# Layer scale on one core: blocks of 60, 60 and 8 rows in place of 8, 60 and 60, and the first 7.9 MB load goes ahead of gamma

## The chip, the cores and the metric

The kernel runs on one core of a Trainium2 chip. The metric is the device time of one execution in microseconds (us). Before the change the median of three runs is 119.92 us (119.86 to 119.98). The profiled execution took 119.96 us, of which 118.6 us lie between its first and its last instruction; the profile calls this the span, and every position in time below counts from its start.

## The reference

```
B, S, D = 1024, 16, 512
x, y:  bfloat16 [B, S, D]        gamma: bfloat16 [D]
def reference(x, y, gamma):
    return x + gamma * y
```

There is one multiplication and one addition for each element. x and y are 16.8 MB each and so is the output: 33.56 MB are read and 16.78 MB are written. No element is used twice.

## The kernel before, in words

The 16,384 rows of 512 elements are spread over the 128 partitions, so that each partition owns 128 rows of 1 KB. `BLOCKS` cuts these 128 rows in three blocks, here of 8, 60 and 60 rows. Inside a block each partition's rows lie one after the other in memory, so one transfer of a block is 128 pieces of contiguous memory, of 8 KB each for the 8-row block (1 MB in all) and of 60 KB each for a 60-row block (7.9 MB in all). All of y has a place of its own in on-chip memory (`y_sb`, 128 rows), and the result is written over it. x has a buffer of 75 rows (`x_sb`), so the rows of x share slots, and a later load of x has to wait for an addition that frees its slots.

Nothing is planned by a scheduler: the order is written out by hand in four lists.

- `SP` is the list of the loads, which the Sync engine issues in this order. `('y', 8, 68)` is rows 8 to 68 of y, and the fourth entry of an x load is the slot in `x_sb` where it begins. A load of x waits on the semaphore `s_add` for the additions that free its slots (L132).
- `ACT` is the list of the Scalar engine's queue: the load of gamma (1 KB, L129), then three stores (L138). A store waits for the additions on its rows. The first store also waits for `s_go`, which TensorE gives when the load named in `RELEASE`, the last big load of x, has landed.
- `DVE` is the list of VectorE's work on the pieces in `PIECES`: 'm' multiplies a piece of y by gamma in place (L180), 'a' adds x to it (L189). Blocks and pieces have the same edges, except that one 60-row block is cut in pieces of 15 and 45 rows.
- `EARLY` says how many entries of the two queues are moved to the very front of the program, ahead of the barrier with which the engines begin. In the kernel before these are the first two loads of y.

After the early loads the Sync queue waits at its third entry, the Scalar queue waits before gamma, and VectorE waits before its first multiplication. TensorE releases all three when the load named in `HOLD`, the 1 MB of y, has landed (`s_held`, L149). Then gamma is loaded as one row into `gamma_row`. TensorE multiplies it by a column of ones, which copies it to all partitions of PSUM (L152), and VectorE casts it into `gamma_sb` (L154). From there the list `DVE` runs.

At the end the Sync engine waits for all additions and all stores.

Of the kernel before, what the change touches and what calls it, by code (L numbers as in the profile page):

```python
# [3 lines left out]

BLOCKS = [8, 60, 60]

PIECES = [8, 15, 45, 60]


SP = [
    ('y', 0, 8),
    ('y', 8, 68),
    ('x', 8, 68, 0),
    ('y', 68, 128),
    ('x', 68, 128, 15),
    ('x', 0, 8, 0),
]
ACT = [('g',), ('s', 8, 68), ('s', 68, 128), ('s', 0, 8)]  # L20

EARLY = (2, 0)

HOLD = ('y', 0, 8)

RELEASE = ('x', 68, 128, 15)

DVE = [('m', 0), ('m', 1), ('m', 2), ('a', 2), ('a', 1), ('m', 3), ('a', 3), ('a', 0)]
MULT, ADD = mybir.AluOpType.mult, mybir.AluOpType.add


def _take(sem, n, eng):


    return eng.wait_ge(sem, n).then_inc(sem, -n)  # L35


def kernel(
    tc: tile.TileContext,
    x: bass.AP,  # L40
    y: bass.AP,
    gamma: bass.AP,
    out: bass.AP,
):

    nc = tc.nc
    P = nc.NUM_PARTITIONS
    tc.close()  # L50
    tc.compile()  # L51

    xf = x.flatten_outer_dims()
    yf = y.flatten_outer_dims()
    of = out.flatten_outer_dims()
    N, D = xf.shape
    rows = N // P
    n = len(PIECES)
    assert sum(PIECES) == rows
    starts = [sum(PIECES[:c]) for c in range(n + 1)]  # L60
    dt = xf.dtype
    edges = [sum(BLOCKS[:c]) for c in range(len(BLOCKS) + 1)]
    assert edges[-1] == rows

    def rows_of(t, a, b):

        c = max(c for c in range(len(BLOCKS)) if edges[c] <= a)
        assert b <= edges[c + 1]
        block = t[P * edges[c] : P * edges[c + 1]].rearrange("(p n) d -> p n d", p=P)
        return block[:, a - edges[c] : b - edges[c], :]  # L70

    gamma_row = nc.alloc_sbuf_tensor("gamma_row", [1, D], dt).ap()
    ones_row = nc.alloc_sbuf_tensor("ones_row", [1, P], dt).ap()
    gamma_sb = nc.alloc_sbuf_tensor("gamma_sb", [P, D], dt).ap()
    y_sb = nc.alloc_sbuf_tensor("y_sb", [P, rows, D], dt).ap()
    x_loads = [w for w in SP + ACT if w[0] == "x"]
    y_loads = [w for w in SP + ACT if w[0] == "y"]
    stores = [w for w in SP + ACT if w[0] == "s"]
    for loads in (x_loads, y_loads, stores):
        assert sum(w[2] - w[1] for w in loads) == rows  # L80
    x_rows = max(w[3] + w[2] - w[1] for w in x_loads)
    x_sb = nc.alloc_sbuf_tensor("x_sb", [P, x_rows, D], dt).ap()
    gamma_ps = nc.alloc_psum_tensor("gamma_ps", [P, D], mybir.dt.float32).ap()

    sem = nc.alloc_semaphore
    s_gamma, s_ones, s_ps, s_dve = sem("s_gamma"), sem("s_ones"), sem("s_ps"), sem("s_dve")
    s_load = {w: sem("s_" + "_".join(map(str, w[:2]))) for w in x_loads + y_loads}
    s_held = {nc.sync: sem("s_held_sp"), nc.scalar: sem("s_held_act"), nc.vector: sem("s_held_dve")}
    s_add, s_go, s_rel, s_end, s_out = sem("s_add"), sem("s_go"), sem("s_rel"), sem("s_end"), sem("s_out")
    added = [a for kind, *a in DVE if kind == "a"]  # L90
    order = {a[0]: k for k, a in enumerate(added)}

    def meets(a, b, c, d):
        return a < d and c < b

    def pieces_of(a, b):
        return [c for c in range(n) if meets(starts[c], starts[c + 1], a, b)]

    def x_at(row):
        return next(w[3] + row - w[1] for w in x_loads if w[1] <= row < w[2])  # L100

    def frees(w):

        c = set()
        for v in x_loads[: x_loads.index(w)]:
            lo, hi = max(v[3], w[3]), min(v[3] + v[2] - v[1], w[3] + w[2] - w[1])
            if lo < hi:
                c |= set(pieces_of(v[1] + lo - v[3], v[1] + hi - v[3]))
        return sorted(c)

    early = []

    def ring(eng, what, n_early):

        known, went = 0, False
        for k, w in enumerate(what):
            kind = w[0]
            if k == n_early:
                _take(s_held[eng], 1, eng)
            need = frees(w) if kind == "x" else pieces_of(w[1], w[2]) + list(w[3:]) if kind == "s" else []  # L120
            need = max((order[c] + 1 for c in need), default=0)
            if kind == "s" and not went:
                _take(s_go, 1, eng)
                went = True
            if need > known:
                eng.wait_ge(s_add, need)
                known = need
            if kind == "g":
                i = eng.dma_start(out=gamma_row, in_=gamma.unsqueeze(0)).then_inc(s_gamma, 16)  # L129
            elif kind == "x":  # L130
                to = x_sb[:, w[3] : w[3] + w[2] - w[1], :]
                i = eng.dma_start(out=to, in_=rows_of(xf, w[1], w[2])).then_inc(s_load[w], 16)  # L132
            elif kind == "y":
                r = slice(w[1], w[2])
                i = eng.dma_start(out=y_sb[:, r, :], in_=rows_of(yf, w[1], w[2])).then_inc(s_load[w], 16)
            else:
                r = slice(w[1], w[2])
                i = eng.dma_start(out=rows_of(of, w[1], w[2]), in_=y_sb[:, r, :]).then_inc(s_out, 16)  # L138
            if k < n_early:
                early.append(i.ins)  # L140

    ring(nc.sync, SP, EARLY[0])
    ring(nc.scalar, ACT, EARLY[1])


    nc.vector.memset(ones_row, 1.0).then_inc(s_ones, 1)  # L146
    _take(s_load[HOLD], 16, nc.tensor)
    for s_one in s_held.values():
        nc.tensor.sem_inc(s_one, 1)  # L149
    _take(s_ones, 1, nc.tensor)  # L150
    _take(s_gamma, 16, nc.tensor)
    nc.tensor.matmul(gamma_ps, ones_row, gamma_row, start=True, stop=True).then_inc(s_ps, 1)  # L152
    _take(s_ps, 1, nc.vector)
    nc.vector.tensor_copy(out=gamma_sb, in_=gamma_ps).then_inc(s_dve, 1)  # L154
    _take(s_dve, 1, nc.vector)

    _take(s_load[RELEASE], 16, nc.tensor)
    nc.tensor.sem_inc(s_go, 1)
    nc.tensor.sem_inc(s_rel, 1)

    landed, open_mults = set(), 0

    def need(loads, c):
        for w in loads:
            if w not in landed and meets(starts[c], starts[c + 1], w[1], w[2]):
                if w == RELEASE:
                    _take(s_rel, 1, nc.vector)
                elif w == HOLD:
                    _take(s_held[nc.vector], 1, nc.vector)
                else:  # L170
                    _take(s_load[w], 16, nc.vector)
                landed.add(w)

    for kind, *args in DVE:
        c = args[0]
        yt = y_sb[:, starts[c] : starts[c + 1], :]
        if kind == "m":
            need(y_loads, c)
            g = gamma_sb[:, None, :].to_broadcast([P, PIECES[c], D])
            nc.vector.tensor_tensor(out=yt, in0=yt, in1=g, op=MULT).then_inc(s_dve, 1)  # L180
            open_mults += 1
        else:
            need(x_loads, c)
            if open_mults:
                _take(s_dve, open_mults, nc.vector)
                open_mults = 0
            at = x_at(starts[c])
            xt = x_sb[:, at : at + PIECES[c], :]
            nc.vector.tensor_tensor(out=yt, in0=xt, in1=yt, op=ADD).then_inc(s_add, 1)  # L189


    nc.scalar.sem_inc(s_end, 1)
    _take(s_end, 1, nc.sync)
    _take(s_add, n, nc.sync)
    _take(s_out, 16 * len(stores), nc.sync)

    main = nc.main_func.blocks[0].instructions
    names = {i.name for i in early}
    for b in nc.main_func.blocks[1:]:
        for i in [i for i in b.instructions if i.name in names]:  # L200
            b.instructions.remove(i)
    for k, i in enumerate(early):
        main.insert(1 + k, i)
# [30 lines left out]
```

## Time and profile before

| what | from the profile of before |
|---|---|
| time, median of three | 119.92 us |
| span | 118.6 us |
| VectorE busy | 70.1 us (59%), 10 instructions |
| TensorE busy | 0.6 us |
| memory read and written | 33.56 MB and 16.78 MB |
| multiplication or addition of 60 rows | 16.2 us |
| of 45 rows | 12.2 us |
| of 15 rows | 4.2 us |
| of 8 rows | 2.3 us |
| issue of the 60-row x load (rows 68 to 128) | at 53.60 us |
| issue of the first store | at 77.83 us |

The compute engines are listed with their busy time and its share of the span. The DMA (memory transfer) work is listed apart: 16 DMA engines move all bytes, each transfer is spread over all of them in packets, and a queue is the ordered list of transfers that one issuing engine has handed to them. Queue q1 belongs to the Sync engine and carries the loads of x and y; q10 belongs to the Scalar engine and carries gamma and the stores. A packet here is one partition's piece, 8 KB or 60 KB, or a 4-byte write to a semaphore. The trace records each packet with its start and its duration. What one DMA engine does in the whole kernel is 48 packets of 60 KB and 24 of 8 KB.

### The profile page before, as it was taken

The numbers are of one execution on the slowest core, as the hardware profiler recorded it, in microseconds if no ns is written. First come the engines' busy times: TensorE is split into PE (matmuls) and PEld (weight loads), VectorE is DVE, ScalarE is ACT, GpSimd is POOL, SyncE is SP. The second block draws the span as 40 slices with busy tenths as digits, with TensorE's granted clock in tenths as the row PEclk, the third lists the DMA queues.
The fourth block names the chain that finished last, engine by engine and source line by source line (L and its number), as shares of the span: only waits on it lengthen the run. The fifth ranks groups of instructions, "written<-read, shape, count | busy, mean of one in ns | idle before, by whom it ended". The sixth has DMA issues, their size and how long they took to land. (4 is left out here: it accounts for less than half of the span.)

```text
span 118.6 us, 87 instructions
## 1 busy us (share of the span) xinstructions
PE 0.6 (0%) x1; PEld 0.1 (0%) x1; DVE 70.1 (59%) x10; POOL 0.2 (0%) x4
## 2 busy tenths in 40 slices
PE   0001000000000000000000000000000000000000
PEld 0000000000000000000000000000000000000000
DVE  0000720199999399999499999569999950000000
POOL 0000000000000000000000000000000000000000
DMA  5999799779779879879977977897997797797787
GB/s 182 503 560 435 331 394 601 331 331 663 331 331 642 352 331 621 373 331 394 601 331 331 663 331 331 384 633 331 414 580 331 331 663 331 331 663 331 331 367 318
DMA packets 1298, 50.33 MB, mean 424 GB/s; under 512 B 145, under 2 KB 146, under 8 KB 146
## 3 DMA queue, kind: packets, MB, share of 16 engines
q1 hardware_dynamic: 864, 33.55, 65.8%
q10 hardware_dynamic: 434, 16.78, 32.7%
HBM read 33.56 MB, written 16.78 MB: 424 GB/s over the span
## 5 line engine op out<-in xcount | busy, mean ns | idle before, releaser
L180 DVE TENSOR_TENSOR y_sb<-y_sb,gamma_sb 128x4096 bf16<-128x4096 bf16 (+3 forms) x4 | 34.7, 8690 | 9.7 <-DVEq L35 9.7
L189 DVE TENSOR_TENSOR y_sb<-x_sb,y_sb 128x23040 bf16<-128x23040 bf16 (+3 forms) x4 | 34.6, 8688 | 4.5 <-DVEq L35 4.5
L154 DVE CAST gamma_sb<-gamma_ps 128x512 bf16<-128x512 f32 x1 | 0.7, 692 | 10.1 <-DVEq L35 10.1
L146 DVE MEMSET ones_row<- 1x128 bf16 x1 | 0.2, 165 | 2.0 <-PEq L51 2.0
L152 PE MATMUL gamma_ps<-gamma_row,ones_row 1*128 1x512 bf16 x1 | 0.6, 578 | 11.6 <-PEq L35 11.6
L152 PEld LDWEIGHTS gamma_ps<-gamma_row,ones_row 1*128 1x128 bf16 x1 | 0.1, 100 | 11.5 <-issue 11.5
L218 POOL MEMSET const-uint8-127<- 128x1 uint8 x1 | 0.1, 102 | 0.0
L218 POOL MEMSET const-bfloat16-1.0<- 128x1 bf16 x1 | 0.1, 101 | 0.0
L218 POOL MEMSET const-float32-0.0<- 128x1 f32 x1 | 0.1, 98 | 0.2 <-issue 0.2
L218 POOL MEMSET const-float32-1.0<- 128x1 f32 x1 | 0.1, 98 | 0.0
## 6 DMA issues: line engine op xcount, KB each, us to landing
y_sb<-in_y_dram SPq DMA_DIRECT2D x2, 7680.0 KB, 38.2
x_sb<-in_x_dram SPq DMA_DIRECT2D x2, 7680.0 KB, 29.9
out_dram<-y_sb ACTq DMA_DIRECT2D x2, 7680.0 KB, 21.0
y_sb<-in_y_dram SPq DMA_DIRECT2D x1, 1024.0 KB, 4.9
x_sb<-in_x_dram SPq DMA_DIRECT2D x1, 1024.0 KB, 22.3
out_dram<-y_sb ACTq DMA_DIRECT2D x1, 1024.0 KB, 22.1
gamma_row<-in_gamma_dram ACTq DMA_DIRECT2D x1, 1.0 KB
```

The lines of the kernel that those rows point to most:

```text
L146: nc.vector.memset(ones_row, 1.0).then_inc(s_ones, 1)
L152: nc.tensor.matmul(gamma_ps, ones_row, gamma_row, start=True, stop=True).then_inc(s_ps, 1)
L154: nc.vector.tensor_copy(out=gamma_sb, in_=gamma_ps).then_inc(s_dve, 1)
L180: nc.vector.tensor_tensor(out=yt, in0=yt, in1=g, op=MULT).then_inc(s_dve, 1)
L189: nc.vector.tensor_tensor(out=yt, in0=xt, in1=yt, op=ADD).then_inc(s_add, 1)
L218: nc = _bacc.Bacc("TRN2", target_bir_lowering=False, num_devices=1)
```

## The change

The first load becomes a 60-row block of y, alone at the front of the program. gamma no longer waits for a load of y; it goes out as soon as the Scalar engine has passed the barrier at the start. The other five loads wait until gamma has landed. The 8-row block moves from the front to the end of the list of loads. So the load named in `RELEASE`, which opens the stores, is now followed by two 1 MB loads in place of one, and VectorE multiplies and adds the 8-row piece last.

The purpose is to have gamma on the chip early, with work for the DMA engines meanwhile, and to let the stores be released while small loads are still to be moved.

```diff
-BLOCKS = [8, 60, 60]
+BLOCKS = [60, 60, 8]
-PIECES = [8, 15, 45, 60]
+PIECES = [15, 45, 60, 8]
 SP = [
-    ('y', 0, 8),
-    ('y', 8, 68),
-    ('x', 8, 68, 0),
-    ('y', 68, 128),
-    ('x', 68, 128, 15),
-    ('x', 0, 8, 0),
+    ('y', 0, 60),
+    ('x', 0, 60, 0),
+    ('y', 60, 120),
+    ('x', 60, 120, 15),
+    ('y', 120, 128),
+    ('x', 120, 128, 0),
 ]
-ACT = [('g',), ('s', 8, 68), ('s', 68, 128), ('s', 0, 8)]
-EARLY = (2, 0)
-HOLD = ('y', 0, 8)
-RELEASE = ('x', 68, 128, 15)
-DVE = [('m', 0), ('m', 1), ('m', 2), ('a', 2), ('a', 1), ('m', 3), ('a', 3), ('a', 0)]
+ACT = [('g',), ('s', 0, 60), ('s', 60, 120), ('s', 120, 128)]
+EARLY = (1, 0)
+AHEAD = 1
+RELEASE = ('x', 60, 120, 15)
+DVE = [('m', 0), ('m', 1), ('a', 1), ('a', 0), ('m', 2), ('a', 2), ('m', 3), ('a', 3)]
...
-            if k == n_early:
-                _take(s_held[eng], 1, eng)
+            if eng is nc.sync and k == AHEAD:
+                _take(s_held, 1, eng)
...
     nc.vector.memset(ones_row, 1.0).then_inc(s_ones, 1)
-    _take(s_load[HOLD], 16, nc.tensor)
-    for s_one in s_held.values():
-        nc.tensor.sem_inc(s_one, 1)
     _take(s_ones, 1, nc.tensor)
     _take(s_gamma, 16, nc.tensor)
+    nc.tensor.sem_inc(s_held, 1)
     nc.tensor.matmul(gamma_ps, ones_row, gamma_row, start=True, stop=True).then_inc(s_ps, 1)
...
                 if w == RELEASE:
                     _take(s_rel, 1, nc.vector)
-                elif w == HOLD:
-                    _take(s_held[nc.vector], 1, nc.vector)
                 else:
                     _take(s_load[w], 16, nc.vector)
```

## The prediction, made before the changed kernel was run

> **What bounds the kernel now.** I read the page from its second part on: the span in 40 slices, then the DMA queues, then the timeline, and last the packet records of the places where the order of transfers changes.
>
> ```profile
> DVE  0000720199999399999499999569999950000000
> DMA  5999799779779879879977977897997797797787
> GB/s 182 503 560 435 331 394 601 331 331 663 331 331 642 352 331 621 373 331 394 601 331 331 663 331 331 384 633 331 414 580 331 331 663 331 331 663 331 331 367 318
> q1 hardware_dynamic: 864, 33.55, 65.8%
> q10 hardware_dynamic: 434, 16.78, 32.7%
> HBM read 33.56 MB, written 16.78 MB: 424 GB/s over the span
> ```
>
> VectorE has holes, DMA has none. The two queues together are busy for 65.8 + 32.7 = 98.5% of 16 engines' span, 116.9 of 118.6 us. The swing between 331 and 663 GB/s comes from counting a packet where it ends. In the packet records a 60 KB packet takes 2.267 us, load or store, and the next starts 2.264 us after it; an 8 KB packet takes 0.309, the next starting 0.306 later. Each engine's work is therefore 48 x 2.264 + 24 x 0.306 = 108.7 + 7.3 = 116.0 us. The first packets start at 1.02 us, but those of half the engines need about a microsecond instead of 0.31 and end at 2.05 to 2.31, so the steady rate begins at about 1.74. 1.74 + 116.0 = 117.7; the engines end between 117.83 and 118.26, and the last store is reported 0.35 us later, at 118.61. So nothing between the first packet and the last costs more than half a microsecond, and the bound is the number of bytes at the engines' rate.
>
> ```profile
> 0.00 0.85 SPq L135 DMA_DIRECT2D y_sb<-in_y_dram  x2
> 5.23 0.33 SPq L132 DMA_DIRECT2D x_sb<-in_x_dram  x1
> 5.43 0.52 ACTq L129 DMA_DIRECT2D gamma_row<-in_gamma_dram  x1
> 11.57 0.58 PE L152 MATMUL gamma_ps<-gamma_row,ones_row 1*128 1x512 bf16 x1 [11.57 <-PEq L35]
> 53.60 4.40 SPq L132 DMA_DIRECT2D x_sb<-in_x_dram  x2
> 77.83 19.02 ACTq L138 DMA_DIRECT2D out_dram<-y_sb  x3
> ```
>
> In this timeline the reader is to see how far ahead transfers are issued. The x load of 53.60 waits for an addition; the load before it, of y, lands at 59.35. The stores are issued at 77.83, and the last load's packets end at 79.14 to 79.58 with the first store's following at once: the smallest margin of the kernel, and it just holds. The 12% "issue" in the chain of waits is the chain's lost track behind the stores' transfer, no cost of its own.
>
> **What the Trainium skill says.** "DMA: Bandwidth & Descriptors", section "Where 436 GB/s comes from", puts the ceiling of the 16 engines at 435 GB/s; the trace's 61,440 bytes in 2.264 us are 27.1 GB/s an engine, 434 for 16, which agrees. The same page, "Queues, rings and completion order", says an engine goes round-robin between the queues it has work for, a packet at a time. The trace agrees: gamma's 1 KB packet starts at 8.76 and its semaphore write at 11.07, with one 60 KB load packet in between. The same page, "Latency and other measured facts", gives 0.6 us to the first byte of a transfer issued from Sync or Scalar; here the first packet starts 1.02 us after its issue and the trace's figure is used. That page says nothing of the cost of alternating between stores and loads on one engine.
>
> **The change part by part.** *Bytes and packets:* the same six loads, three stores and gamma, with as many packets of each size. 116.0 us an engine before and after: 0.
>
> *The first load.* It is 60 rows instead of 8. The delay up to 1.74 us is that of the first bytes, which a larger packet has once too: 0. Half the engines showed 0.7 to 1.0 us too much on their first packet, so I allow 0.3 either way. Issuing one early load instead of two spares 0.43 us of Sync's time, hidden by the first load's packets.
>
> *gamma without a hold.* VectorE passes the barrier at 1.99, so gamma is issued at about 2.0 instead of 5.43. It took 6.0 us then from issue to landing (11.43), behind 60 KB packets; the same now lands it at about 8, one packet sooner or later 6 to 10. All that stands behind it fits under y's first load: that is 8 x 2.264 = 18.1 us of packets, to 19.85.
>
> *The hold of five loads until gamma has landed.* Queued behind it on Sync: all other loads; those who wait are the DMA engines and then VectorE. Release to issue took 0.33 us (4.90 to 5.23), issue to first packet 1.0, so x's first packets are ready at about 9.5, 11.5 at worst, against 19.85. Hidden by y's load by over 8 us: 0.
>
> *VectorE.* y lands at 1.74 + 18.1 + 0.35 = 20.2; multiplications of 15 and 45 rows run to 36.7. x lands at 38.3; the additions of 45 and 15 rows run from 38.5 to 50.7 and 54.9. The first frees the second big x load, issued at 50.8, first packet at 51.8; y's second load keeps the engines to 1.74 + 54.3 = 56.1, 4.3 us to spare. The last x load follows at 54.9. The 60-row multiplication runs 56.6 to 72.8. Moving the 8-row multiplication away from the front is free: VectorE was waiting there (7.6 us idle).
>
> *The stores.* The big x load has its last packets at 1.74 + 72.4 = 74.2, lands at 74.55; from landing to store issue was 0.35 (77.48 to 77.83), so issue at 74.9 and first packets ready at about 76.0. By then the 8 packets of y's 8 rows are done but for two; with x's 8, ten 8 KB packets an engine remain. Before, one 1 MB load covered this delay, barely; now two do. Nothing was lost there before, so nothing is gained. From 76.0 an engine alternates 2.26 us of store with 0.31 of load: the last x load, landing 2.5 us after the big one before, now lands at about 76 + 10 x 2.57 = 102. The 60-row addition (75.2 to 91.4) lets the second store go at 91.4, while the first lasts to about 97: 5 us to spare. The 8-row multiplication follows the big addition; its addition waits for x, ending at 104.5, and its store is wanted at 115.3: over 10 us to spare. The sum stays 0.
>
> *Alternation itself.* No row of before shows a load packet after a store packet on one engine. From below: 0, since load to store at 79.14 and load to gamma to load at 8.76 (46 ns) show no gap. From above: each of ten loads exposes a start as at the beginning, 0.7 us, 7 us in all. I take 0: the engine's rate is the same for both directions, and the one switch between queues back to a load cost nothing. For the range I keep 0.1 us a switch, 1 us.
>
> Sum: 119.92 + 0 = 119.9 us.
>
> **The rivals.** *First: loads between stores are slow.* For it: never seen before, and the kernel holds its stores until the big loads are in, which avoids nearly all mixing. Against it: free switches elsewhere. With 0.1 us for each of ten packets: 119.9 + 1.0 = 120.9 us, slower. *Second: a cleaner start or equal engines.* Engines differ by 0.43 us at the end, and the last has 0.28 us too much on 8 KB and 0.11 on 60 KB packets; if these go, it ends 0.39 earlier, 119.5 us, faster. For it: the excess is at the first transfer, which is replaced. Against it: the second to last engine ends only 0.09 earlier. *Third: a gap in the queue*, from gamma landing late or the second x load going out after 56. It needs a delay of 4 to 8 us; a gap of 1 us gives 120.9. The margins speak against it.
>
> **How the numbers follow.** No change 50%, slow alternation 26%, cleaner start 20%, a gap 4%. The likeliest is 119.9. The range runs from 119.5, the second rival, to 120.9, the first and the third at their stated size; left out are larger costs of alternation, about 13%, and little below. Faster by over 0.2% (under 119.68): 0.22, the second rival and a margin. Slower (over 120.16): 0.28, since the alternation can cost less than that. Same: 0.50.
>
> **What would show it.** Right: both queues again at 98 to 99%, 60 KB packets at 2.267, first store issued near 75, the 8 rows of x landing near 102 with no harm, last packet at about 118.2. Wrong: 8 KB packets longer than 0.31 us between stores, or gaps ahead of them (first rival); last packet before 117.9 (second); an empty slice near 20 or 56 us (third).

## The result, and the profile after

The changed kernel takes 121.10 us (median of six runs, 120.90 to 121.27) against 119.89 us (119.84 to 119.99). The ratio is 1.0098, with a 95% interval of 1.0085 to 1.0111: 1.2 us slower. The forecast was 119.9 us, with a range up to 120.9. So the time is outside the range, on the side of the first rival.

The page of the changed kernel, its span and its DMA queues (packets, MB, share of 16 engines' span):

```profile
span 119.8 us, 84 instructions
q1 hardware_dynamic: 864, 33.55, 66.1%
q10 hardware_dynamic: 434, 16.78, 32.4%
HBM read 33.56 MB, written 16.78 MB: 420 GB/s over the span
```

The number of packets and of bytes is that of before, and there is still no hole: 98.5% of the engines' span. But 66.1% of 119.8 is 79.2 us for the Sync queue's loads, against 65.8% of 118.6, 78.0 us, before. With the durations of the packet records added up it is 79.2 against 78.1 us an engine, and 38.8 us in both kernels for the other queue, that of the stores. The same load packets keep the engines about 1.1 us longer, and that is nearly the whole difference of 1.2 us. So the time is to be looked for in load packets that last longer, not in gaps.

Its timeline, with the lines that answer to those shown of before:

```profile
0.00 0.37 SPq L135 DMA_DIRECT2D y_sb<-in_y_dram  x1
1.43 0.52 ACTq L129 DMA_DIRECT2D gamma_row<-in_gamma_dram  x1
9.10 0.58 PE L150 MATMUL gamma_ps<-gamma_row,ones_row 1*128 1x512 bf16 x1 [9.10 <-PEq L35]
9.14 0.33 SPq L132 DMA_DIRECT2D x_sb<-in_x_dram  x1
51.53 0.33 SPq L132 DMA_DIRECT2D x_sb<-in_x_dram  x1
75.75 21.46 ACTq L138 DMA_DIRECT2D out_dram<-y_sb  x3
```

The issues come nearly as forecast. gamma goes out at 1.43, somewhat earlier, and lands at 8.77; what follows is up to 0.9 us late: the second big x load goes out at 51.53, while y's second load is moving until 57, and the stores are issued at 75.75. None of these waits stops the engines.

Where packets last longer is seen by dividing the rate by the share in a stretch. The share is the mean busy share of the 16 engines, and a packet is counted where it starts, so a share above 1 only means that packets which start in the stretch last beyond its end. (The forecast has packets counted where they end. But the view gives 922 GB/s between 1 and 2 us here, and the first 60 KB packets end from 3.87 us on.) GB/s divided by the share is the rate of busy engines: 424 to 434 wherever packets have their usual length, the lower figure for 8 KB in 0.309 us and the higher for 60 KB. The stretches of the changed kernel (start and end, length, engines' busy times, clock, DMA share, GB/s):

```profile
0.00:2.30 2.30, 0.00 (x0) 0.00 (x0) 0.17 (x1) 0.20 (x4) 1.00 1.32 427
20.00:74.20 54.20, 0.00 (x0) 0.00 (x0) 48.61 (x5) 0.00 (x0) 1.00 0.99 428
77.00:80.00 3.00, 0.00 (x0) 0.00 (x0) 3.00 (x1) 0.00 (x0) 1.00 1.14 373
80.00:116.00 36.00, 0.00 (x0) 0.00 (x0) 16.69 (x3) 0.00 (x0) 1.00 1.00 434
```

From 20 to 74 us it is 428 / 0.99 = 432, from 80 on 434. In the three microseconds from 77 it is 373 / 1.14 = 327, and at the start 427 / 1.32 = 323. These are the two places. The kernel before has these lines for the start and for the change from loads to stores:

```profile
0.00:2.30 2.30, 0.00 (x0) 0.00 (x0) 0.17 (x1) 0.20 (x4) 1.00 0.45 110
76.70:79.60 2.90, 0.00 (x0) 0.00 (x0) 1.48 (x1) 0.00 (x0) 1.00 1.63 695
```

At the change it is 695 / 1.63 = 426, so nothing is slow there. Its start is slow as well, 110 / 0.45 = 244, but over fewer bytes: what the packets of the first 4 us take above 0.309 and 2.267 us adds up to 0.44 us an engine before and 0.78 after.

The packet records show the two places packet by packet. At the start, the first 60 KB packets of the 16 engines end between 3.87 and 4.76 us. Taking off 2.267, the engines have their usual rate as if from 1.61 to 2.49; before, eight packets of 8 KB led to 1.73 to 2.11 in the same sense. The latest of the engines is 0.4 us later than the latest before. Near 77 us the packets of one engine are these (start, duration in ns):

```
before, x's 8 rows, store issued at 77.83     after, x's 8 rows, store issued at 75.75
76.688  309                                   76.734  309   load
 ... six more loads at 309                    77.039  309   load
78.830  309   last load                       77.345  525   load
79.141 2267   first store                     77.866  568   load
                                              78.431  587   load
                                              79.015  502   load
                                              79.514  455   load
                                              79.965  309   load
                                              80.271 2267   first store
```

All 16 engines have two to five such packets. The excess over 0.309 is 0.42 to 1.15 us an engine, 0.80 in the mean. In the kernel before it is zero. The last packets of the 16 engines end between 118.61 and 119.37 us, against 117.82 to 118.25 before: 0.9 us later in the mean, and 1.1 us at the last engine, which sets the time.

### The profile page after: what moved, and what is told of

Same layout as the page of the kernel before. It is cut to its first block, busy times and chain, and to the rows that moved or that the text cites. A ratio compares the mean times of both kernels' runs of the same rounds, so it can differ in the third digit from the quotient of the medians.

```text
span 119.8 us, 84 instructions
## 1 busy us (share of the span) xinstructions
PE 0.6 (0%) x1; PEld 0.1 (0%) x1; DVE 70.1 (59%) x10; POOL 0.2 (0%) x4
## 3 DMA queue, kind: packets, MB, share of 16 engines
q1 hardware_dynamic: 864, 33.55, 66.1%
## 5 line engine op out<-in xcount | busy, mean ns | idle before, releaser
L176 DVE TENSOR_TENSOR y_sb<-y_sb,gamma_sb 128x7680 bf16<-128x7680 bf16 (+3 forms) x4 | 34.7, 8688 | 12.4 <-DVEq L35 12.4
```

## The experiments

Theory A: a store that comes while loads are still to be moved slows these loads. Theory B: sixteen 8 KB load packets in a row are slow by themselves. Theory C: all of the loss is at the head. To these the forecast's first rival adds a cost of each alternation. The time of the kernel before in each comparison was 119.90 to 119.95 us.

### The stores released one load later

```diff
-RELEASE = ('x', 60, 120, 15)
+RELEASE = ('y', 120, 128)
```

> The changed kernel, with the stores released by the second-last load (8 rows of y, landing at 77.88 us) instead of the last big one (75.40). Theory A, the store descriptors that reach the engines while 8 KB load packets are still moving slow those packets: first store issued near 78.2, the 8 KB packets all at 0.309 us again, and 0.6 to 0.9 us of the loss of 1.2 us goes away, so about 120.3 us (a start gap of up to 0.4 us on some engines included). Rival B, sixteen 8 KB load packets in a row are slow in themselves from about the eleventh on: the packets stay at 0.4 to 0.7 us and the time at 121.1 or above. Rival C, all of the loss is at the head: 121.1.

Measured: 120.42 us, ratio 1.0043 (1.0030 to 1.0056). The first store is issued at 78.27, and the stretch before it reads:

```profile
77.00:79.10 2.10, 0.00 (x0) 0.00 (x0) 2.10 (x1) 0.00 (x0) 1.00 1.03 433
```

That is 433 / 1.03 = 420, near the 424 of 8 KB packets: the sixteen are at 0.31 us, the excess is 0.01 us an engine. B falls. With the stores' start mended, 0.5 us over before remains, and the rest of the 1.2 us, some 0.7, went with it. The first 60 KB packets end between 3.89 and 4.82 us here as well: what is left is the head's.

### Eight rows first

```diff
 SP = [
+    ('y', 120, 128),
     ('y', 0, 60),
...
     ('x', 60, 120, 15),
-    ('y', 120, 128),
     ('x', 120, 128, 0),
-EARLY = (1, 0)
+EARLY = (2, 0)
-AHEAD = 1
+AHEAD = 2
```

> The changed kernel with its 8 rows of y as the first load, issued early together with the 60 rows of y, so that one 8 KB load is left after the release; gamma is still issued at once and the other loads still wait for it. If the loss is a slow first 60 KB packet (0.2 to 0.4 us) plus the slow 8 KB packets at the stores' start (0.8), both are gone: 119.9 us, engines end at 118.3. If gamma's early issue into the first descriptors is what delays the head: 120.2 to 120.3. If the address layout of the blocks (60, 60, 8) is to blame: 121.1.

Measured: 119.95 us, ratio 0.9999 (0.9991 to 1.0007). Both losses are gone, with blocks of 60, 60 and 8 rows, with gamma issued at once, and with the other loads held until it has landed. None of these three parts of the change costs or brings anything. What costs is which load is first and how many loads are left when the stores begin.

### The kernel before, with its stores released one load earlier

```diff
-    ('x', 68, 128, 15),
+    ('x', 68, 120, 15),
+    ('x', 120, 128, 67),
-RELEASE = ('x', 68, 128, 15)
+RELEASE = ('x', 68, 120, 15)
```

> The kernel before with its last big x load cut in 52 and 8 rows and the stores released by the 52 rows, so that two 8 KB loads are left after the release, behind the head of before. Theory A (stores disturb 8 KB loads): packets of 0.4 to 0.7 us again, 0.7 to 0.9 us more than before, about 120.7 us. Rival C (all at the head): 119.9. Rival B (a long row of 8 KB packets): slow as well, so this run only tells A and B from C, and gives the size without the changed head.

Measured: 121.13 us, ratio 1.0098 (1.0082 to 1.0113), 0.4 us more than expected. The loss is made with the head of before, so C falls:

```profile
76.90:79.80 2.90, 0.00 (x0) 0.00 (x0) 2.04 (x1) 0.00 (x0) 1.00 1.33 449
```

449 / 1.33 is 338. The excess is 0.81 us an engine in the mean, that of the changed kernel. But it is uneven, 0.48 to 1.26 us by engine: the engines end 0.9 us later than before in the mean, and the last one, which sets the time, 1.2 us later (119.41 against 118.25). That is where the 0.4 us beyond the expectation lie. Why the engines lose unequally no run shows.

### The stores beside a big load

```diff
-RELEASE = ('x', 60, 120, 15)
+RELEASE = ('y', 60, 120)
```

> The changed kernel with the stores released by the second 60-row load of y (landing 57.2 us), so that the first store of 60 KB packets runs beside the big x load of 60 KB packets. If switching between store and load packets costs something each time, the 60 KB load packets between stores are longer than 2.267 us by 0.1 us or more, over all eight of them. If only the arrival of the store's descriptors costs, one or two packets an engine are longer near 59 us and the rest are at 2.267. The kernel itself is slower by some 8 to 12 us, since the second store waits for a later addition.

Measured: 132.19 us (one run), some 11 us of it the wait for a later addition, in which every engine is idle for 10.3 to 11.8 us. The stores are issued at 57.65. These are the stretches from there on:

```profile
58.90:62.00 3.10, 0.00 (x0) 0.00 (x0) 3.10 (x1) 0.00 (x0) 1.00 1.11 357
64.30:94.00 29.70, 0.00 (x0) 0.00 (x0) 11.08 (x2) 0.00 (x0) 1.00 0.96 416
```

First 357 / 1.11 = 322, then 416 / 0.96 = 433. On most engines the last load packet before the first store packet is the long one, of 2.7 to 3.5 us; the excess is 0.95 us an engine in the mean. After that 60 KB load and store packets alternate, each at 2.267. This alternation is free: the engine pays once, when the stores begin.

### One queue for all

```diff
     ('x', 120, 128, 0),
+    ('s', 0, 60), ('s', 60, 120), ('s', 120, 128),
 ]
-ACT = [('g',), ('s', 0, 60), ('s', 60, 120), ('s', 120, 128)]
+ACT = [('g',)]
```

> The changed kernel with its three stores on the Sync queue behind the last load, so that stores and loads are in one queue and the store is issued at the same time as before. Theory A1, an engine loses about 0.8 us when a second queue becomes active while the first still has packets unread: no second queue here, the 8 KB packets stay at 0.309 us, the loss at the stores' start is gone, and only the head's 0.45 us stays: 120.4 us. Rival A2, the loss is the first store's (its first write to memory, its descriptors) whatever its queue: 8 KB packets of 0.5 to 0.7 us again and 121.1 us.

Measured: 121.38 us, ratio 1.0115 (1.0101 to 1.0129). The stretch from 77 us:

```profile
77.00:80.00 3.00, 0.00 (x0) 0.00 (x0) 3.00 (x1) 0.00 (x0) 1.00 1.14 359
```

It is 315, as slow as with two queues. Here the stores stand behind the loads in the same queue, and loads ahead of them are slowed all the same. My theory that a second queue's start costs is wrong.

### The head: the first load cut, and gamma later

These three start from the kernel with the stores released later, 120.42 us. First the same 60 rows at the same addresses, in two loads:

```diff
-    ('y', 0, 60),
+    ('y', 0, 8),
+    ('y', 8, 60),
-EARLY = (1, 0)
+EARLY = (2, 0)
-AHEAD = 1
+AHEAD = 2
```

> The kernel of e1_stores_later (120.42 us) with its first load of 60 rows cut in 8 and 52 rows at the same addresses, both issued early. If a large first packet is what spreads the engines at the start (ends of the first 60 KB packets from 3.87 to 4.76 us in the changed kernel), the spread falls to 0.4 us as in the kernel before, and the time to about 120.0. If it is the distance of 60 KB between the partitions' first pieces in memory, the spread and 120.4 stay.

Measured: 119.98 us, ratio 1.0004 (0.9996 to 1.0013). The head's loss is gone, so it is not where the first packets lie in memory. Then the cut at 30 rows in place of 8:

> e6_first_load_cut_8_52 (119.98 us) with the cut at 30 rows. If the cost at the head grows with the size of the first packets, this one, with 30 KB, lies between 8 KB (119.98) and 60 KB (120.42), near 120.15; the 61,440 bytes of the first 60 rows' two packets end with a spread of about 0.6 us over the engines. If any cut cures it: 119.95 and a spread of 0.4 us or less.

Measured: 120.28 us, ratio 1.0030 (1.0018 to 1.0042): between the two, nearer to 60 rows and not clearly apart from them. As both runs issue two loads early, it is the size of the first packets that matters and not the number of early loads. Last, gamma held back by a fill of 15 rows on VectorE:

```diff
             if kind == "g":
+                _take(s_delay, 1, eng)
...
+    nc.vector.memset(x_sb[:, 60:75, :], 0.0).then_inc(s_delay, 1)
```

> The kernel of e1_stores_later (120.42 us) with gamma's issue held back by one fill of 15 rows of the x buffer on VectorE, 2 to 8 us. If gamma's issue at 1.42 us, amid the first packets, is what spreads the engines at the start: first packets of 60 KB end between 3.8 and 4.2, time about 120.0. If it is not: 120.4 and the same spread from 3.9 to 4.8.

Measured: 120.54 us, ratio 1.0053 (1.0040 to 1.0066). gamma is issued at 5.66 instead of 1.42 and the loss is as large: gamma's early issue is not its cause.

### A smaller first store

```diff
-ACT = [('g',), ('s', 0, 60), ...
+ACT = [('g',), ('s', 0, 8), ('s', 8, 60), ...
```

> The changed kernel with its first store cut in 8 and 52 rows. If the loss at the stores' start is the time in which the first store packet is read ahead while loads are still moving, a first packet of 8 KB instead of 60 KB loses less: 0.3 us or less an engine instead of 0.8, and about 120.6 us. If the loss belongs to the start of the second queue whatever the packet, it stays at 0.8 and the time at 121.1.

Measured: 121.36 us, ratio 1.0127 (1.0109 to 1.0144), with longer 8 KB load packets before the first store again. The excess is 0.62 us an engine in the mean, a little less, but the last engine ends at 119.62, later than in the changed kernel. Small store packets do not avoid the loss.

### The last load on the Scalar queue

```diff
     ('y', 120, 128),
-    ('x', 120, 128, 0),
 ]
-ACT = [('g',), ('s', 0, 60), ...
+ACT = [('g',), ('x', 120, 128, 0), ('s', 0, 60), ...
```

> The changed kernel with its last load, 8 rows of x, on the Scalar queue ahead of the stores; it is issued at about 55.6 us, beside the big loads on the Sync queue, and one 1 MB load is left when the stores come. If anything that joins loads which are still moving costs an engine 0.8 us, 60 KB packets near 57 to 61 us are longer by 0.5 to 1.3 us. If only a store does that, all 60 KB packets there stay at 2.267, and at the stores' start few 8 KB packets are longer, since only one load is left: loss 0.45 us in all, about 120.4 us.

Measured: 120.44 us (one run). From 54 to 74 us the x load's 8 KB packets alternate with 60 KB load packets, and the stretch shows 441 / 1.02 = 432:

```profile
54.00:74.00 20.00, 0.00 (x0) 0.00 (x0) 17.79 (x2) 0.00 (x0) 1.00 1.02 441
```

All of these packets have their usual length. A load that joins loads costs nothing, unlike a store. And the 0.7 us are gone, since one 1 MB load in place of two is left when the stores come.

### A store ahead of the stores

Is it the kernel's first store that costs? A store of gamma, 1 KB a partition, was put at 10.6 us:

```diff
...
+            elif kind == "w":
+                _take(s_warm_go, 1, eng)
+                i = eng.dma_start(out=rows_of(of, 120, 121), in_=gamma_sb[:, None, :]).then_inc(s_warm, 16)
...
```

> The changed kernel with a store of 128 KB (one row a partition, of gamma, overwritten by the last store) issued at about 11 us amid the first loads. If the loss belongs to the kernel's first store on an engine, the 60 KB load packets near 12 to 17 us take the extra 0.5 to 1 us, and the 8 KB packets before the first big store are at 0.309; time 121.1 to 121.4. If it comes whenever stores begin beside unread loads, the 8 KB packets near 77 to 80 us are at 0.4 to 0.7 us as before, and little is seen at 12 us; time 121.4 with the 0.3 us of the added store.

Measured: 121.54 us, ratio 1.0137 (1.0122 to 1.0153). The first stretch is the one in which that store begins (its packets run from 15.10 to 30.19 us), the second that in which the big stores begin:

```profile
6.00:19.00 13.00, 0.58 (x1) 0.10 (x1) 0.69 (x1) 0.00 (x0) 1.00 1.06 456
77.40:80.50 3.10, 0.00 (x0) 0.00 (x0) 3.10 (x1) 0.00 (x0) 1.00 1.31 457
```

430, then 349. The small store costs the loads nothing (from 12 to 36 us the 60 KB load packets have an excess of 0.01 us an engine), and the loss of the big ones stays (0.76 us an engine). It is not the first store as such. Then a store of 1 MB, 8 rows of zeros, at 5.67 us:

```diff
...
+                i = eng.dma_start(out=rows_of(of, 120, 128), in_=x_sb[:, 60:68, :]).then_inc(s_warm, 16)
...
```

> The changed kernel with a 1 MB store (8 rows a partition, 8 KB packets, of zeros from the x buffer, overwritten by the last store) issued at about 5.7 us beside the first loads, and the same start of the big stores as in the changed kernel. A 128 KB store of 1 KB packets cost nothing there. If the loss is the reading ahead of a store's data while loads are unread, this one costs each engine 0.3 to 0.8 us on 60 KB load packets between 7 and 14 us, and the big stores cost 0.8 again near 78. If the loss needs 60 KB store packets or 8 KB load packets, nothing is seen at 7 to 14 us. The time is 2.45 us longer by the bytes of the store, near 123.6 without a second loss, near 124.2 with it.

Measured: 124.0 us (one run), with 2.45 us of it the bytes of the added store. Its stretches:

```profile
18.00:21.00 3.00, 0.00 (x0) 0.00 (x0) 0.00 (x0) 0.00 (x0) 1.00 0.99 371
80.70:82.50 1.80, 0.00 (x0) 0.00 (x0) 1.80 (x1) 0.00 (x0) 1.00 1.62 692
```

375 at 18 us, then 427 at the place where the changed kernel had 327. The 60 KB load packets beside the 1 MB store lose 0.6 us an engine in the mean between 8 and 21 us, two thirds of it in the packets that start from 18.5 on. On every engine the longest, 2.52 to 2.98 us, is the eighth and last packet of y's first load. The store's packets go on to 28.1 us, and beside the later ones the load packets are at 2.267. The big stores, issued at 79.38 with 2.6 to 3.7 us of loads left on 15 of the engines, then cost 0.01. That was not expected: in this one run the loss is paid once, by the first store of some size. It is read from the packets; the time lies between the 123.6 and 124.2 of the expectation, as one engine ends at 122.28 and the others by 121.78.

### Two rows first

The run with eight rows first is changed once more:

```diff
-    ('y', 120, 128),
+    ('y', 120, 122),
+    ('y', 122, 128),
     ('y', 0, 60),
...
-EARLY = (2, 0)
+EARLY = (3, 0)
-AHEAD = 2
+AHEAD = 3
```

> e2_small_load_first (119.95 us) with its first load of 8 rows cut in 2 and 6 rows, all issued early. The order at the head so far: 60 KB packets first +0.45 us, 30 KB +0.35, 8 KB 0. If smaller first packets go on helping, the engines start together a little earlier and it takes 119.8 or less, better than both kernels; if the start is then only the delay of the first bytes, 119.95.

Measured: 120.64 us, ratio 1.0079 (1.0048 to 1.0109). (One of its six runs took 121.85.) With 2 KB packets engines run out of packets at the head: between 1 and 8 us an engine is idle for 0.76 us in the mean, against 0.38 with eight rows first. So 8 rows, as in the kernel before, were the best of the sizes tried (2, 8, 30, 60), and no version beat the kernel before.

## Why the prediction was wrong

**What held.** The bound: both queues fill 98.5% of the engines' span before and after. The waits: gamma, the hold of five loads and the second x load stayed hidden with margins of several microseconds, so the third rival played no part. VectorE's order was free. The sum of issues and landings up to the stores was right within 0.9 us. Its start of the steady rate, 1.74, is that of the earliest engines; the sixteen lie at 1.73 to 2.11 in the kernel before, so the 117.7 us worked out from it is below every end that the trace has.

**The first load, put at 0.** The step said that the delay of the first bytes comes once, whatever the packet's size, and left 0.3 us for it. It measured 0.45 us: 120.42 with 60 rows first, 119.98 with the same rows cut 8 and 52. The term was in the forecast, and too small. Why a large first packet makes some engines late isn't settled; addresses and gamma are ruled out.

**The stores' start and alternation, put at 0.** This is the step that failed most. It took from the load-to-store change at 79.14 that a switch is free. In that trace the loads are all but done when the stores come: they end 1.3 to 1.7 us after the stores' issue, so it could not show what stores do to loads that are left. In the changed kernel the loads needed more than 4 us beyond the issue, and the first longer packets start 1.5 us after it. The stores' start cost 0.8 us an engine, some 0.7 us of the time. The first rival's time, 120.9, is near, but by chance: there is no 0.1 us for each of ten alternations, there is one payment, and alternation, where it was seen, is free. Nor did an engine alternate from 76.0 on, as the step has it: the first store packets start from 79.85 on, 4.1 us after the issue (1.3 us before the change), and on every engine at least 15 of the sixteen 8 KB load packets went ahead of them. So the last x load was not drawn out to 102 us; it had landed by 85.53. Why so many loads go ahead no run shows.

**The range** took the two unknown costs as alternatives. They came together: 0.45 + 0.7 is 1.15 of the 1.2 us. These sizes are differences of whole times, each set by its last engine, and do not simply add: behind the head of the kernel before, the stores' start alone cost 1.2 us.

**What it is in the engine** was only argued. Loads ahead of a store in the same queue are slowed, a load that joins costs nothing, 128 KB of stores cost nothing, 1 MB of stores pays and the later stores are then free. This would fit an engine that reads a store's data ahead, once, out of the rate that the loads then lack; by an estimate from the packet records, 0.8 us x 27 GB/s, some 20 KB. No run looked at the engine's reading itself, and two things speak against it as it stands: by the same estimate the 8 KB an engine of the 128 KB store should have cost 0.3 us and cost 0.01, and the loss beside the 1 MB store falls mostly on the last packet of a load, some 10 us after that store's first packets. The cause inside the engine stays open.

## What to carry to other kernels

In a kernel bound by transfers, look at what is still to be moved at the moment when the first stores become ready: here one 1 MB load left cost nothing and two cost 0.7 to 1.2 us, with no hole in the DMA row to show it. The rate divided by the busy share shows it, and so does a queue that takes longer for the same packets. A transition that is free in the trace is free under the conditions of that trace only; where the change alters what lies on either side of it, its cost is unknown, and two unknown costs in one change belong in the range as a sum.

## What the runs showed of the hardware that was not expected

- Stores that began beside unfinished loads took 0.6 to 1.0 us from a DMA engine in the mean of the sixteen (single engines 0.1 to 1.3 us), at the start only. After that, 60 KB load and store packets alternated at 2.267 us each. A store of 128 KB took 0.01 us from the loads, and loads with 0.9 to 1.7 us left at the stores' issue lost nothing.
- It made no difference whether the stores were in a queue of their own or behind the loads in the same one (rates of 327 and 315 GB/s in the same three microseconds).
- The size of the first packets showed in the time over the kernel before: 2 KB 0.7 us, 8 KB nothing, 30 KB 0.4 us, 60 KB 0.5 us. With 2 KB the engines were idle in between; why 30 and 60 KB make engines late is open.
